# A linear-attention kernel and a maxout layer: two stages in turn, then one software pipeline

## The chip, the cores and the metric

The kernel runs on one core of one Trainium2 chip. The metric is the device time of one execution in microseconds (us), as the median of several executions. Profiles are single executions of the same kernel; their span is a few us shorter than the measured time. An execution counts as slow if it is over 1.5% above the fastest one of its kernel, and comparisons use fast runs alone.

Engines in the profile: PE is the TensorE (matmuls), PEld its weight loads, DVE the VectorE, ACT the ScalarE, POOL the GpSimd and SP the SyncE, which here only issues transfers. "Clock" is the share of its full speed that the record grants to the TensorE; the record is a list of entries, and the views count time without an entry as full (the kernel before has none until 215.3 us, and its attention reads 1.00).

## The reference

A gated linear attention over 4 batches, 8 heads, 768 positions and 48 elements a head, then a two-way maxout layer (384 to 1024 to 384) over the 3072 tokens.

```python
f = 1.0 / (1.0 + np.exp(-f_logit))
for t in range(S):                       # S = 768
    state = f[:, :, t, :, None] * state + einsum('bhd,bhe->bhde', k[:, :, t], v[:, :, t])
    y[:, :, t] = einsum('bhd,bhde->bhe', q[:, :, t], state)
x = y.transpose(0, 2, 1, 3).reshape(B * S, H * D)          # 3072 x 384
out = np.maximum(x @ w1, x @ w2) @ w_out                   # w1, w2: 384 x 1024
```

Both kernels cut the time axis into 6 chunks of 128 positions; a tile is one chunk of one batch with all heads, so there are 24 tiles. In a chunk the decays become cumulative sums (`cum`), q and k are scaled with their exponentials, and y is a masked product inside the chunk (`at`) plus q times the carried state; `sadd` updates the state.

## The kernel before

It has two stages. The first goes through the tiles (cut to the lines that the argument touches):

```python
for c in range(nch):
    for b in range(B):
        ...                                        # loads: q, k, f by SP, v by POOL (with a cast)
        nc.scalar.activation(tmp, ft2, AF.Exp, bias=0.0, scale=-1.0)
        nc.scalar.activation(ell_c, tmp, AF.Ln, bias=1.0, scale=1.0)
        nc.tensor.matmul(out=cumL, lhsT=ut, rhs=ell_c, start=True, stop=True)
        ...                                        # F_dec, F_inv: Exp of cumL; qp = q*F_dec, kp = k*F_inv on POOL
        for p in range(npiece):                    # 8 transposes
            nc.tensor.transpose(out=trq[:, p * C:(p + 1) * C], in_=qp[:, p * C:(p + 1) * C], identity=ident)
            ...
        nc.vector.tensor_copy(trSe, trq[0:D, :])       # even heads
        nc.vector.tensor_copy(trSo, trq[64:64 + D, :]) # odd heads, moved to partitions 0 to 47
        for j in range(H):
            nc.tensor.matmul(out=at_all[:, j, :], lhsT=kpT(j), rhs=qpT(j), start=True, stop=True)
        nc.vector.tensor_mul(at_m, at_all, ut_big)
        for j in range(H):
            nc.tensor.matmul(out=yps[:, ds], lhsT=at_m[:, j, :], rhs=v_c[:, ds], start=True, stop=False)
            nc.tensor.matmul(out=yps[:, ds], lhsT=qpT(j), rhs=state[:, j, :], start=False, stop=True)
        ...                                        # sadd, new state
        nc.scalar.copy(x_sbuf[:, ti, :], yps)
```

The second loads and casts the weights, transposes x in 72 pieces, and then:

```python
for ffb in range(FGRP):                            # 8
    for ts in range(ntsub):                        # 6 groups of 512 tokens
        ...                                        # h1 += w1.T x, h2 += w2.T x: 3 matmuls each, one PSUM buffer each
        nc.scalar.copy(gslc, h1)
        nc.vector.tensor_max(gslc, gslc, h2)
for i in range(n_tok_tiles):
    ...                                            # ops: 8 matmuls over gT and wo, copy, store
```

## Time and profile before

| | before |
|---|---|
| time, median of 3 (range) | 327.97 us (327.60 to 328.39) |
| span of the profiled run | 324.3 us |
| attention, weights and transposes, layer | 190.5, 21.5, 112.3 us |

The prediction below quotes the page's busy line, slices, stages and costliest groups. One view that it did not read closely is the list of groups on PE. Columns: line, engine and operation, output<-inputs, shapes, count; then busy us and mean ns of one; then the idle time before and its releaser.

```profile
L196 PE MATMUL h<-xT,w 128*128 128x512 bf16 x144 | 39.8, 387 | 0.3 <-DVE xT L183 0.3
...
L209 PE MATMUL ops<-wo,gT 128*128 128x384 bf16 x192 | 33.2, 326 | 0.0
L121 PE MATMUL trq<-ident,kp 128*128 128x128 bf16 x96 | 25.0, 313 | 3.2 <-POOL kp L106 3.2
...
L136 PE MATMUL at_all<-trSe 48*128 48x128 bf16 x96 | 22.7, 303 | 0.0
...
L94 PE MATMUL cumL<-ell_c,ut 128*128 128x384 bf16 x24 | 11.7, 487 | 30.1 <-ACT ell_c L91 25.5 <-ACT F_inv L99 4.5
```

A matmul's duration is longer than its share of the engine, since neighbours overlap (at_all lasts 0.31 us where starts lie 0.11 apart), but like can be compared with like. L94 and L209 are alike: both stream 384 columns in 128*128. One averages 487 ns in attention, the other 326 ns in the layer. The spacings that the prediction reads say the same: 0.107 us for 128 columns in attention, 0.216 for 512 in the layer, which is 0.84 ns a column against 0.42. So the array does not run alike in the two. This difference decides the case, and it stood in the profile beforehand.

### The profile page before, as it was taken

The numbers are of one execution on the slowest core, as the hardware profiler recorded it, in microseconds if no ns is written. First come the engines' busy times: TensorE is split into PE (matmuls) and PEld (weight loads), VectorE is DVE, ScalarE is ACT, GpSimd is POOL, SyncE is SP. The second block draws the span as 40 slices with busy tenths as digits, with TensorE's granted clock in tenths as the row PEclk, the third lists the DMA queues.
The fourth block names the chain that finished last, engine by engine and source line by source line (L and its number), as shares of the span: only waits on it lengthen the run. The fifth ranks groups of instructions, "written<-read, shape, count | busy, mean of one in ns | idle before, by whom it ended". The sixth has DMA issues, their size and how long they took to land.

```text
span 324.3 us, 4531 instructions
## 1 busy us (share of the span) xinstructions
PE 253.9 (78%) x1728; PEld 150.3 (46%) x1728; DVE 155.3 (48%) x267; ACT 148.7 (46%) x241; POOL 75.2 (23%) x93
## 2 busy tenths in 40 slices
PE   0258857967867697789879787688999998999995
PEld 0136635644555365456546554333333333345663
DVE  0145443645545365564546638934444444444442
ACT  3973668467927965784687010023333333330000
POOL 6353235432433351364434200000000000000000
PEclk9999999999999999999999999999999999999999
DMA  9947465856665687667674209500000000012443
GB/s 147 120 80 114 51 87 78 142 63 85 98 99 73 79 117 111 85 89 114 90 99 25 14 8 379 196 2 0 0 0 2 0 0 0 2 50 97 161 157 121
DMA packets 105156, 26.23 MB, mean 81 GB/s; under 512 B 100272, under 2 KB 104368, under 8 KB 105136
## 3 DMA queue, kind: packets, MB, share of 16 engines
q1 hardware_dynamic: 80176, 23.60, 31.8%
q0 software_dynamic: 24960, 2.36, 13.9%
q8 instruction: 13, 0.21, 0.3%
q14 instruction: 7, 0.06, 0.1%
HBM read 23.59 MB, written 4.72 MB: 87 GB/s over the span
## 4 chain that ended last, share of the span: by engine, by line
issue 37%; PE 30%; POOL 17%; DVE 12%; ACT 2%; DMA 1%; DVEq 0%; POOLq 0%; ACTq 0%
PE h L199 12%; PE ops L209 10%; DVE gT L203 8%; POOL kp L106 7%; POOL vt L81 6%; POOL qp L103 3%; PE h L196 3%; PE tps L182 2%; DVE xT L183 2%; PE yps L143 1%; PE yps L144 1%; DMA vt<-in_v_dram 1%; ACT L91 1%; POOL ut_big L51 1%; DVE wo L173 1%
## 5 line engine op out<-in xcount | busy, mean ns | idle before, releaser
L202 ACT CAST gT<-h 128x512 bf16<-128x512 f32 x48 | 28.1, 585 | 71.1 <-PE h L196 71.1
L203 DVE TENSOR_TENSOR gT<-gT,h 128x512 bf16<-128x512 bf16 x48 | 33.0, 687 | 48.0 <-PE h L199 48.0
L138 DVE TENSOR_TENSOR at_m<-at_all,ut_big 128x1024 bf16<-128x1024 f32 x24 | 29.4, 1224 | 43.7 <-PE at_all L136 43.7
L199 PE MATMUL h<-xT,w 128*128 128x512 bf16 x144 | 39.5, 382 | 7.4 <-DVE gT L203 7.4
L143 PE MATMUL yps<-vt,at_m 128*128 128x48 bf16 x192 | 42.8, 223 | 1.3 <-DVE at_m L138 1.3
L103 POOL TENSOR_TENSOR qp<-qt,F_dec 128x384 bf16<-128x384 f32 x24 | 23.7, 988 | 72.6 <-ACT F_dec L98 69.9
L196 PE MATMUL h<-xT,w 128*128 128x512 bf16 x144 | 39.8, 387 | 0.3 <-DVE xT L183 0.3
L94 PE MATMUL cumL<-ell_c,ut 128*128 128x384 bf16 x24 | 11.7, 487 | 30.1 <-ACT ell_c L91 25.5
L158 ACT CAST x_sbuf<-yps 128x384 bf16<-128x384 f32 x24 | 11.5, 477 | 50.0 <-PE yps L144 49.6
L209 PE MATMUL ops<-wo,gT 128*128 128x384 bf16 x192 | 33.2, 326 | 0.0
L91 ACT ACT_TABLE_LOAD x24 | 30.8, 1283 | 0.4
L81 POOL DMA_DIRECT2D vt<-in_v_dram x24 | 22.6, 941 | 34.5 <-PE yps L144 31.1
L149 PEld LDWEIGHTS <-kp 128*48 128x48 bf16 x192 | 9.7, 128 | 44.0 <-DMA vt<-in_v_dram 35.4
L124 DVE COPY trSe<-trq 48x1024 bf16<-48x1024 bf16 x24 | 16.4, 681 | 25.9 <-PE trq L121 25.9
L199 PEld LDWEIGHTS <-w 128*128 128x128 bf16 x144 | 14.1, 98 | 29.9 <-issue 18.4
L121 PE MATMUL trq<-ident,kp 128*128 128x128 bf16 x96 | 25.0, 313 | 3.2 <-POOL kp L106 3.2
L149 PE MATMUL sadd<-vt,kp 128*48 128x48 bf16 x192 | 12.7, 217 | 18.7 <-DMA vt<-in_v_dram 18.0
L143 PEld LDWEIGHTS <-at_m 128*128 128x128 bf16 x192 | 20.1, 105 | 12.0 <-DVE at_m L138 1.6
L106 POOL TENSOR_TENSOR kp<-kt,F_inv 128x384 bf16<-128x384 f32 x24 | 25.4, 1056 | 0.1
L152 DVE TENSOR_TENSOR tmpS<-state,sadd 48x384 f32<-48x384 bf16 x24 | 13.1, 546 | 25.1 <-PE sadd L149 24.9
L209 PEld LDWEIGHTS <-gT 128*128 128x128 bf16 x192 | 18.8, 98 | 13.7
L120 PE MATMUL trq<-ident,qp 128*128 128x128 bf16 x96 | 24.1, 303 | 0.0
(42 smaller groups left out, 370.6 us busy)
## 6 DMA issues: line engine op xcount, KB each, us to landing
qt<-in_q_dram SPq DMA_DIRECT2D x24, 192.0 KB, 2.7
kt<-in_k_dram SPq DMA_DIRECT2D x24, 192.0 KB, 3.2
ft<-in_f_logit_dram SPq DMA_DIRECT2D x24, 192.0 KB, 3.7
out_dram<-obuf SPq DMA_DIRECT2D x24, 192.0 KB, 1.9
w_f<-in_moe_w_dram SPq DMA_DIRECT2D x2, 1536.0 KB, 8.4
vt<-in_v_dram POOLq DMA_DIRECT2D x24, 96.0 KB, 3.7
wo_f<-in_moe_w_out_dram SPq DMA_DIRECT2D x1, 1536.0 KB, 14.1
```

The lines of the kernel that those rows point to most:

```text
L81: nc.gpsimd.dma_start(out=vt, in_=v[b, :, sl, :].rearrange("h p d -> p h d"))
L91: nc.scalar.activation(ell_c, tmp, AF.Ln, bias=1.0, scale=1.0)
L103: nc.gpsimd.tensor_mul(qp.rearrange("p (h e) -> p h e", h=H)[:, :, :D], q_c.rearrange("p (h d) -> p h d", h=H), F_dec.rearrange("p (h d) - ...
L106: nc.gpsimd.tensor_mul(kp.rearrange("p (h e) -> p h e", h=H)[:, :, :D], k_c.rearrange("p (h d) -> p h d", h=H), F_inv.rearrange("p (h d) - ...
L121: nc.tensor.transpose(out=trq[:, HDP + p * C:HDP + (p + 1) * C], in_=kp[:, p * C:(p + 1) * C], identity=ident)
L138: nc.vector.tensor_mul(at_m, at_all, ut_big)
L143: nc.tensor.matmul(out=yps[:, ds], lhsT=at_m[:, j, :], rhs=v_c[:, ds], start=True, stop=False)
L196: nc.tensor.matmul(out=h1, lhsT=w1[:, j, ffb * C:(ffb + 1) * C], rhs=xT[:, j, tslice], start=(j == 0), stop=(j == DGRP - 1))
L199: nc.tensor.matmul(out=h2, lhsT=w2[:, j, ffb * C:(ffb + 1) * C], rhs=xT[:, j, tslice], start=(j == 0), stop=(j == DGRP - 1))
L202: nc.scalar.copy(gslc, h1)
L203: nc.vector.tensor_max(gslc, gslc, h2)
L209: nc.tensor.matmul(out=ops, lhsT=gT[:, ffb, i * C:(i + 1) * C], rhs=wo[:, ffb, :], start=(ffb == 0), stop=(ffb == FGRP - 1))
```

## The change

The intent is one pipeline instead of two stages. A slot is one tile; in it PE makes `at` of tile n, y and the state of tile n-1, `cum` of tile n+2 and the transposes of tile n+1, and between them up to two pieces `d` of the layer (h for 128 of the 1024 columns and 512 tokens) and one piece `o` (the output of 128 tokens). The order on each engine is fixed by the program. With it come:

- maxout as `relu(x(w1-w2)) @ wo + x (w2 wo)`, which halves the h matmuls and drops the maximum; `w2 wo` (m2) is computed once, on PE;
- x made transposed by y's matmuls; heads 6 and 7 then lie in the wrong block, so w1 and w2 are loaded in a changed row order and six small copies per group of four tiles move the rows of x;
- heads in pairs on partitions 0 to 63 and 64 to 127 (zero-padded), and one preloaded activation table.

```diff
-        # attention stage, then weights and x's transposes, then the layer
+    nc.scalar.preload_act_table_set("natural_log_exp_and_others")
+    def load_rows(dst, w):                       # w1, w2 in the row order of x
+        hd = w.rearrange("(h d) f -> d h f", d=D)
+        nc.sync.dma_start(out=dst[0:D, :, :], in_=hd[:, 0:6:2, :])
+        nc.sync.dma_start(out=dst[DP:DP + D, :, :], in_=hd[:, 1:6:2, :])
+        for r in range(2):
+            ...                                  # 16 partitions each
+    def stage_A_pe(n):
+        for j in range(NP):
+            for r in range(2):
+                rows = slice(r * DP, r * DP + D)
+                nc.tensor.matmul(out=ps[r][:, j, :], lhsT=t[rows, 0, j, :], rhs=t[rows, 1, j, :],
+                                 start=True, stop=True)
+    def stage_Y_act(n):
+        nc.scalar.copy(xT[c][:, :, b * C:(b + 1) * C], ys.pop(n))
+        if b == B - 1:
+            for r in range(2):
+                for i in range(KT):              # six copies of 16 partitions
+                    nc.sync.dma_start(out=x[r * DP + D:(r + 1) * DP, i, :],
+                                      in_=x[r * DP + 16 * i:r * DP + 16 * (i + 1), KT, :])
+    def piece_d(g, ff):
+        ...                                      # 3 matmuls into h
+        nc.scalar.activation(gT[g][:, ff, :], ps, AF.Relu)
+    def piece_o(g, b):
+        ...                                      # 3 matmuls with m2, then 8 with wo
+    slot = -3
+    while slot < n_tiles + 2 or queue:
+        n = slot
+        if n % B == 1 and 4 < n <= n_tiles + 1:  # layer pieces of a finished group
+            g = (n - 5) // B
+            queue += [("d", g, ff) for ff in range(FG)] + [("o", g, b) for b in range(B)]
+        ...                                      # load(n+5), E(n+3), A(n), Y(n-1), D(n-1), C(n+2),
+        ...                                      # one d, T(n+1), one d, one o
```

In the prediction "mode" means the rows by columns of the array that a matmul uses, as the timeline prints them (48*128, 128*128, ...); each change of it is put at the 0.13 us more that the prediction reads between at_all and trq.

> **What bounds the kernel now.** I read first the busy time of each engine and the slices on the page, then the table by stage, then the groups, and last the timeline for the spacing of matmuls. From the page, busy time and the slices (tenths busy, each 8.1 us):
>
> ```profile
> PE 253.9 (78%) x1728; PEld 150.3 (46%) x1728; DVE 155.3 (48%) x267; ACT 148.7 (46%) x241; POOL 75.2 (23%) x93
> ...
> PE   0258857967867697789879787688999998999995
> ...
> ACT  3973668467927965784687010023333333330000
> POOL 6353235432433351364434200000000000000000
> ...
> DMA  9947465856665687667674209500000000012443
> GB/s 147 120 80 114 51 87 78 142 63 85 98 99 73 79 117 111 85 89 114 90 99 25 14 8 379 196 2 0 0 0 2 0 0 0 2 50 97 161 157 121
> ```
>
> PE is the busiest, yet not filled, and three regimes follow one another: attention (to slice 23), where ACT, POOL and DMA work; weights and transposes of x (24 to 26); the layer, where DMA is idle. The stage table (stretch, its length, busy us of each engine, clock, DMA share, GB/s) says how long each is:
>
> ```profile
> 21.80:190.50 168.70, 132.18 (x1115) 90.60 (x1115) 89.73 (x117) 105.03 (x171) 63.73 (x65) 1.00 0.63 85
> 190.50:212.00 21.50, 15.40 (x88) 9.26 (x89) 16.63 (x75) 0.48 (x1) 0.00 (x0) 1.00 0.60 220
> 212.00:290.00 78.00, 70.54 (x297) 29.14 (x298) 31.92 (x49) 26.92 (x46) 0.00 (x0) 1.00 0.02 6
> 290.00:324.30 34.30, 30.65 (x185) 17.79 (x183) 14.21 (x25) 1.17 (x2) 0.00 (x0) 1.00 0.35 127
> ```
>
> Attention takes 168.7 us for 23 tiles, 7.3 each, and no engine is full in it: ACT 62%, PE 78% by spans that overlap. It is bound by waits around short buffers (the largest by pairs of engine: POOL's qp for F_dec on ACT 69.9 us, ACT's x_sbuf for yps 49.6, DVE's at_m for at_all 43.7, POOL's issue of v for yps 31.1). The groups show what fills ACT, and the two evacuations of the layer:
>
> ```profile
> L203 DVE TENSOR_TENSOR gT<-gT,h 128x512 bf16<-128x512 bf16 x48 | 33.0, 687 | 48.0 <-PE h L199 48.0
> L143 PE MATMUL yps<-vt,at_m 128*128 128x48 bf16 x192 | 42.8, 223 | 1.3 <-DVE at_m L138 1.3
> L91 ACT ACT_TABLE_LOAD x24 | 30.8, 1283 | 0.4
> ```
>
> With the smaller groups (16, 6 and 3) there are 49 table loads, 62.9 us, 42% of ACT's busy time. In the timeline (start, duration) starts tell what a matmul really takes, since durations overlap:
>
> ```profile
> 179.57 0.22 PE L144 MATMUL yps<-state,trSo 48*128 48x48 bf16 x1
> 179.72 0.22 PE L143 MATMUL yps<-vt,at_m 128*128 128x48 bf16 x1
> 179.88 0.22 PE L144 MATMUL yps<-state,trSe 48*128 48x48 bf16 x1
> ...
> 182.06 0.31 PE L136 MATMUL at_all<-trSe 48*128 48x128 bf16 x1
> 182.17 0.31 PE L136 MATMUL at_all<-trSo 48*128 48x128 bf16 x1
> 182.41 0.29 PE L120 MATMUL trq<-ident,qp 128*128 128x128 bf16 x1
> ```
>
> So yps costs 0.153 us a matmul where weights of 128 and of 48 rows alternate, although it streams 48 columns; at_all, all of one kind, costs 0.107 with 128 columns; a change of kind (at_all to trq) costs 0.24, some 0.13 more. By the same reading sadd takes 0.056 each (8 in 0.45), h 0.216 (3 in 0.65) and ops 0.1625 (8 per 1.30 us). In the layer one round of h1 and h2 takes 1.655 us for 1.29 of matmuls: each PSUM buffer of h is single and PE waits for its evacuation.
>
> [...]exp and ln are both in natural_log_exp_and_others, so one load serves both;[...] the input streams at 147 GB/s with DMA full (slice 0), the weights at 379. The change leaves that.
>
> **The change, part by part.** *Removed:* 48 of 49 table loads, about 61.6 us of ACT; 144 matmuls of h (144 x 0.216 = 31 us of PE); 48 maxima (33 us of DVE); 72 transposes and copies of x (7.7 us of PE at 0.107); the serial stage of 21.5 us; the alternation in y; v's issue on POOL. *Added:* x times m2 inside o, 72 x 0.1625 = 11.7 us of PE; preparation of w2T and m2, 24 x 0.107 + 24 x 0.1625 = 6.5 us; wd on POOL: kp takes 1.0 us for 384 elements, so 3072 take about 8 us, once. *Moved:* both regimes are interleaved in one order per slot (a slot is one tile). The listing of the changed order gives, for a full slot on PE:
> - transposes 8 x 0.107 = 0.86; at 8 x 0.107 = 0.86;
> - y 16 x 0.08 = 1.28 (estimate between sadd's 0.056 and at's 0.107, for 64 weight columns and 128 streamed); sadd 8 x 0.06 = 0.5;
> - cum 0.16 plus four sums of about 0.1 = 0.56;
> - d 6 x 0.216 = 1.30; o 11 x 0.1625 = 1.79;
> - four changes of mode, 4 x 0.13 = 0.5.
>
> Sum 7.65. The even and odd heads now sit on different rows of the array and may overlap, worth up to 0.6 in at and y; I choose **7.4 us**. Beside it ACT needs 2 x 0.52 + 0.59 + 2 x 0.485 + 0.17 + 2 x 0.585 = 3.9, DVE two at_m halves of 0.69, trs 0.69, tmp_s 0.4, vb 0.3, ob 0.56 = 3.3, POOL 2.05 + 0.7 = 2.8, DMA 786 KB at 150 GB/s = 5.2 plus the output's 0.5. So PE sets the steady slot, and results are used a slot later than made[...]; I expect few waits there.
>
> The start is set by DMA. Four tiles lie ahead of the weights: 4 x 5.2 + 2 = 23 us. The weights, 4.7 MB, take 13 us at the 379 GB/s of before; in the new row order pieces of 48 and 16 partitions may be slower, I take 17. So f of tile 4 lands at about 41; slot 1 hangs there, because ACT runs the slot's Exp before the copies behind it. From there a tile lands each 5.2 us: slot 5 starts at about 58, loses about 4 to m2 (3.9) and to wd on POOL, ahead of kp of tile 6; slots 5 to 7 have no o and take 10, 6, 6. Slot 8 starts at about **86**. Slots 8 to 24: 17 x 7.4 = 126, less 6 since the last four lack sadd, and then cum, transposes, at: **120**. The tail, layer only: four slots of two d and one o (3.1) and three of one o (1.8) = **18**. After the last matmul, 3.7 as now (320.6 to 324.3). Sum 228; the measured time lies 3.7 above the span (327.97 against 324.3): 231.5. I add 2.5 for waits not seen: **234 us**.
>
> **The rivals.** *DMA is the bound throughout:* 24 x 5.2 + 17 + 4.7 MB of output at about 350 GB/s (13) = 155 us plus the tail; under PE's sum, but if small packets go slower in company (85 GB/s at share 0.63 is 135 at full, so 5.8 a tile) the start slips by some 6 us: about 240. *A fixed order turns into waits* (PE blocked on a bank that ACT frees late, ACT blocked behind an Exp that waits for f): nothing is that close in the sums, ACT being half filled; one wait of 0.5 us per slot would give 245, one of 1 us 255. *Modes cost more than I take:* if y and at in 64-row and 64-column tiles run at 0.15 as yps did, a slot gains 1.5 us: 258. *Heads overlap fully* (0.055 each for at and y): slot 6.7, time 222. *The start hides better*, weights at full rate: 229.
>
> **Range and chances.** Slot 7.4 with 0.6 either way is 10 us, the start 7, and waits only add: 218 to 256. Even the worst rival lies 20% under 328, so faster by over 2% is 0.98.
>
> **What would show it.** ACT has one table load; busy ACT about 95 us. PE slices are low up to about 40 us with DMA near full, then 9s from about 85 us to the tail. Starts of the first at_e of successive slots lie 7.0 to 7.8 apart in the middle; at_e to at_o spacing tells about overlap (0.107 or 0.055), the step from Y to sadd and cum about modes. wd on POOL shows 7 to 8 us. The chain that ended last should be PE from o, d and y, with DMA at its beginning. The prediction is wrong if the slots in the middle are paced by something other than PE, if the weights take over 25 us, or if matmuls in small tiles space wider than 0.11.

## The result, and the profile after

| | before | after |
|---|---|---|
| time, median of 4 (range) | 327.79 us (327.54 to 328.39) | 206.52 us (206.28 to 206.89) |
| ratio of fast runs | | 0.6302 (95%: 0.6279 to 0.6325) |
| span of the profiled run | 324.3 us | 204.9 us |
| PE busy | 253.9 us | 141.6 us |

A ratio is the mean time of one kernel's fast runs over the mean of the other's fast runs of the same rounds, so it is not quite the ratio of the medians. The changed kernel is 37% faster, and at 206.5 us it lies below the predicted range of 218 to 256. A later repeat of the unaltered file, beside a later batch of runs, gave 206.81 us (206.14 to 209.44), ratio 0.631.

The page of the changed kernel, busy time and slices (tenths; each slice 5.1 us):

```profile
PE 141.6 (69%) x1452; PEld 85.7 (42%) x1472; DVE 81.6 (40%) x145; ACT 87.6 (43%) x196; POOL 72.3 (35%) x90
...
PE   0257300004464999929999699995999999959993
...
PEclk9999999999999799975999979997999999979999
DMA  6999999999999499958699589795891111111122
GB/s 126 189 186 191 162 163 168 228 242 198 186 187 187 72 187 185 171 97 172 141 176 217 116 167 179 150 224 107 168 196 45 58 42 40 45 55 38 55 95 80
```

There are two regimes: to slice 12 the DMA is full and PE mostly waits; afterwards PE is full apart from four dips. Each dip has a fall of the granted clock beside or after it. Stages of the changed kernel (stretch, length, busy of PE, PEld, DVE, ACT, POOL, clock, DMA share, GB/s; the last two rows are one steady slot and one of the long ones):

```profile
13.19:81.58 68.39, 31.50 (x368) 21.15 (x372) 29.10 (x44) 23.99 (x60) 25.91 (x21) 0.98 1.14 181
...
122.19:127.23 5.04, 4.99 (x63) 3.13 (x64) 3.04 (x6) 3.49 (x8) 2.57 (x3) 1.00 0.87 174
86.62:98.10 11.48, 7.35 (x63) 3.94 (x64) 3.04 (x6) 3.60 (x8) 2.56 (x3) 0.70 0.71 137
```

**The steady slot takes 5.04 us, not 7.4.** Its timeline on PE (start, duration, operation; from the second half of `at`):

```profile
122.31 0.22 PE L178 MATMUL at_e<-trs 48*128 48x128 bf16 x1
122.32 0.22 PE L178 MATMUL at_o<-trs 48*128 48x128 bf16 x1
122.37 0.22 PE L178 MATMUL at_e<-trs 48*128 48x128 bf16 x1
122.37 0.22 PE L178 MATMUL at_o<-trs 48*128 48x128 bf16 x1
122.52 0.41 PE L200 MATMUL y<-trs,state 48*64 48x128 bf16 x8
122.86 0.41 PE L205 MATMUL y<-at_m,vb 128*64 128x128 bf16 x8
123.11 0.29 PE L218 MATMUL sadd<-vb,kp 128*64 128x64 bf16 x8
123.33 0.34 PE L127 MATMUL cum<-ell,ut 128*128 128x384 bf16 x1
...
124.25 0.39 PE L160 MATMUL trp<-ident,kp 128*128 128x128 bf16 x4
124.47 0.39 PE L160 MATMUL trp<-ident,qp 128*128 128x128 bf16 x4
```

Read the starts. Four transposes of 128 columns take 124.47 - 124.25 = 0.22 us, 0.056 each, where the kernel before took 0.107. The starts of successive at_e are also 0.055 apart, each with an at_o beside it. Early in the same run, before the layer joins in, both were slow:

```profile
66.05 0.31 PE L178 MATMUL at_e<-trs 48*128 48x128 bf16 x1
66.06 0.31 PE L178 MATMUL at_o<-trs 48*128 48x128 bf16 x1
66.16 0.31 PE L178 MATMUL at_e<-trs 48*128 48x128 bf16 x1
66.16 0.31 PE L178 MATMUL at_o<-trs 48*128 48x128 bf16 x1
```

Here at_e starts are 0.11 apart and a matmul lasts 0.31 us instead of 0.22: the durations of the kernel before. The mean clock does not show this: it is 0.98 over this first stage and 1.00 over all attention of the kernel before. Most of that time has no entry in the record and is counted as full. In the packed traces the entries begin at 62.5 us here, and in the kernel before only at 215.3 us, 3.2 us after the first h. Where there is an entry, the spacing fits it: 66.05 lies in one of half rate (65.9 to 69.3), and in this run all 111 gaps between transposes under full entries are 55 or 56 ns, all 21 under half entries 106 or 107.

In this run the entries and the spacings agree, then: 106 to 107 ns for 128 columns at half rate, 55 to 56 at full. What misleads is the mean.

**Three slots of the steady part are long**, 11.5, 9.0 and 9.1 us (9.4, 9.0 and 8.8 in the later repeat). The first of them on PE:

```profile
87.93 0.24 PE L130 MATMUL cum<-ones_col,ell 128*128 128x1 bf16 x4
92.04 1.87 PE L258 MATMUL h<-xT,wd 128*128 128x512 bf16 x3 [3.87 <-DMA xT<-xT]
93.70 0.63 PE L160 MATMUL trp<-ident,kp 128*128 128x128 bf16 x4
94.13 0.63 PE L160 MATMUL trp<-ident,qp 128*128 128x128 bf16 x4
```

and what SP, which issues the transfers, did at that time:

```profile
85.93 0.99 SPq L71 DMA_DIRECT2D vt<-in_v_dram  x1
87.02 4.98 SPq L249 DMA_DIRECT2D xT<-xT  x6
```

PE stops 3.87 us for the six copies of xT that the piece `d` needs, and the matmuls after it run at half rate again (four transposes in 0.43 us). SP reaches the copies only after the loads of tile 13, and issuing the six takes it 4.98 us, against a median of 1.9 us from the issue of a copy to its landing.

**The start.** On ACT, the wait for the first input behind the weights ends at 45.36:

```profile
45.36 0.52 ACT L120 ACTIVATE tmp_e<-ft 128x384 f32<-128x384 f32 x1 [26.91 <-DMA ft<-in_f_logit_dram]
```

Slots 1 and 2 begin at 17.38 and 21.48, so a tile lands each 4.1 us, at the page's 186 to 191 GB/s. The weights, which the slices show at 160 to 170 and at last 240 GB/s, hold the queue from about 21 to 44 us: 23 us.

### The profile page after: what moved, and what is told of

The parts are those of the page before. It is cut to its first block, busy times and chain, and to the rows that moved or that the text cites. A ratio compares the mean times of both kernels' runs of the same rounds, so it can differ in the third digit from the quotient of the medians.

```text
span 204.9 us, 3795 instructions
## 1 busy us (share of the span) xinstructions
PE 141.6 (69%) x1452; PEld 85.7 (42%) x1472; DVE 81.6 (40%) x145; ACT 87.6 (43%) x196; POOL 72.3 (35%) x90
## 4 chain that ended last, share of the span: by engine, by line
PE 52%; issue 19%; SPq 9%; DMA 8%; DVE 5%; ACT 3%; POOL 2%; DVEq 0%; POOLq 0%
PE h L258 15%; PE o L268 13%; PE o L265 5%; SPq L249 5%; PE trp L160 4%; SPq L71 4%; DMA xT<-xT 4%; PE at_e L178 3%; PE y L205 3%; PE y L200 3%; PE m2p L295 2%; DMA ft<-in_f_logit_dram 2%; DMA qt<-in_q_dram 2%; PE cum L127 2%; DVE vb L153 1%
## 5 line engine op out<-in xcount | busy, mean ns | idle before, releaser
L258 PE MATMUL h<-xT,wd 128*128 128x512 bf16 x124 | 41.7, 413 | 12.2 <-DMA xT<-xT 10.3
L260 ACT ACTIVATE gT<-h 128x512 bf16<-128x512 f32 x48 | 28.9, 603 | 31.2 <-PE h L258 30.7
L147 POOL TENSOR_TENSOR kp<-kt,f_inv 128x384 bf16<-128x384 f32 x24 | 24.9, 1037 | 39.6 <-ACT f_inv L140 36.0
L168 DVE COPY trs<-trp 128x1024 bf16<-128x1024 bf16 x24 | 16.6, 691 | 54.3 <-PE trp L160 54.3
L268 PE MATMUL o<-wo,gT 128*128 128x384 bf16 x192 | 35.1, 326 | 0.0
L244 ACT CAST xT<-y 128x512 bf16<-128x512 f32 x24 | 14.0, 582 | 29.4 <-PE y L205 29.4
L149 POOL TENSOR_TENSOR qp<-qt,f_dec 128x384 bf16<-128x384 f32 x24 | 24.0, 1000 | 0.0
L186 DVE TENSOR_TENSOR at_m<-at_e,ut 128x512 bf16<-128x512 f32 x24 | 16.4, 685 | 5.7 <-PE at_o L178 5.7
L265 PE MATMUL o<-m,xT 128*128 128x384 bf16 x72 | 16.7, 344 | 0.0
L186 DVE TENSOR_TENSOR at_m<-at_o,ut 128x512 bf16<-128x512 f32 x24 | 16.3, 681 | 0.0
## 6 DMA issues: line engine op xcount, KB each, us to landing
w_f<-in_moe_w_dram SPq DMA_DIRECT2D x4, 576.0 KB, 13.2
```

The lines of the kernel that those rows point to most:

```text
L147: nc.gpsimd.tensor_mul(padded["kp"][n % NB][:, :, 0:D], loaded[n]["k"], f_inv.rearrange("p (h d) -> p h d", h=H))
L149: nc.gpsimd.tensor_mul(padded["qp"][n % NB][:, :, 0:D], loaded[n]["q"], f_dec.rearrange("p (h d) -> p h d", h=H))
L168: nc.vector.tensor_copy(t, ps)
L186: nc.vector.tensor_mul(m[:, r], ps[r], ut4)
L244: nc.scalar.copy(xT[c][:, :, b * C:(b + 1) * C], ys.pop(n))
L258: nc.tensor.matmul(out=ps, lhsT=wd[:, kt, ff * C:(ff + 1) * C], rhs=xT[g][:, kt, :], start=(kt == 0), stop=(kt == KT - 1))
```

## The experiments

The experiments ran in four batches, in which the kernel before took 326.6 to 327.87 us (medians), so each is given with its ratio to the kernel before in the same rounds; for the changed kernel that is 0.6302 and 0.631. "Slot lengths" are differences between the starts of the first at_e of successive tiles in the timeline. The theory after the result was: the spacings that the prediction took from attention were half-rate spacings, and the dense order of the changed kernel runs at full rate. The rival: the new operations (padded pairs, other tiles, another order) are cheaper in themselves.

### All layer pieces after attention (e1)

```diff
-        p = next_piece(n, "d")
+        p = next_piece(n, "d") if n > n_tiles else None     # likewise for "o"; six xT buffers
```

> The changed kernel with all layer pieces moved behind the attention (same instructions, not interleaved; xT gets six buffers). Theory 'clock': [...]it stays at half rate as in the kernel before and in the first 66 us of the changed kernel: transposes 0.106 us apart, a pair of even and odd heads of at 0.105, a 384-column matmul shown as about 0.48. Rival 'shape of the tiles': the fast spacing comes from the new tiles, so transposes stay at 0.056 and pairs of at at 0.055 in attention too. In both, attention is paced by the input at about 4.1 us a tile, ends near 135 us, and the layer adds 48 x 0.65 + 24 x 1.79 = 74 us: about 216 us in all, 4% slower than the changed kernel.

Measured: 235.1 us (231.95 to 236.67), ratio 0.7148. The attention operations are the very ones of the changed kernel, now without the layer between them. Clock in slices and a timeline of PE in attention:

```profile
PEclk9999999999988755555555555559999999999999
```

```profile
102.35 0.59 PE L160 MATMUL trp<-ident,kp 128*128 128x128 bf16 x4
102.72 0.64 PE L160 MATMUL trp<-ident,qp 128*128 128x128 bf16 x4
104.15 0.28 PE L178 MATMUL at_e<-trs 48*128 48x128 bf16 x1 [0.79 <-DVE trs L168]
```

The spacing is back at 0.105 for 128 columns, the record itself grants half, and slots take 4.13 us, the pace at which inputs land. So the operations are not cheaper in themselves; they are cheaper in dense company: PE is busy for 16.08 of 20 us here (80 to 100 us), against 4.99 of 5.04 in the steady slot. The expected total was missed, because attention ended only at 154 us: slot 8 began at 83.5, and sixteen slots of 4.13 us or more follow. Interleaving, by overlap and density together, is worth 29 us here.

### The kernel before with useless matmuls (e7)

```diff
                 yps = ps_y.tile([C, HD], F32, name="yps")
+                for _ in range(12):                          # 384 columns each, overwritten afterwards
+                    nc.tensor.matmul(out=yps, lhsT=ut, rhs=ut_big[:, 0:3, :]..., start=True, stop=True)
```

> The kernel before with twelve extra matmuls of 384 columns a tile into the bank of yps, which the first real matmul overwrites; the result stays right. Theory 'clock': PE is then busy enough for the full rate, transposes and at go from 0.107 to 0.056 apart, the extra matmuls take 0.1625 each, and the time stays near 327 (315 to 335) despite 288 more matmuls. Rival 'shape': the spacing stays 0.107, the extra ones take 0.32 each, and 24 x 3.8 us come on top: 400 or more.

Measured: 323.45 us (319.9 to 328.41), ratio 0.9869 (0.9808 to 0.9931). The groups on PE, the fillers first:

```profile
L142 PE MATMUL yps<-ut_big,ut 128*128 128x384 bf16 x288 | 72.1, 385 | 0.4 <-ACT F_last L115 0.3
...
L136 PE MATMUL at_all<-trSe 48*128 48x128 bf16 x96 | 17.4, 234 | 0.0
L121 PE MATMUL trq<-ident,kp 128*128 128x128 bf16 x96 | 16.9, 233 | 1.9 <-POOL kp L106 1.7
```

288 more matmuls, and the kernel is not slower: PE is 90% busy instead of 78%, a transpose of k takes 233 ns instead of 313, at_all 234 instead of 303, and in the timeline both are spaced 0.056 us wherever the record's entry is full, about 0.107 where it is half. The tiles, pools and shapes of the kernel before are untouched, so this refutes the rival and shows the clock's part. Two limits of it: the alternating yps matmuls went only from 0.153 to 0.127 us, so most of that cost is not the clock, and that it is the change of tile shape, which the prediction named, is the author's reading, which no run separates (in the changed kernel y no longer alternates, and its 16 take 0.59 us); and the time gained by the clock went into the fillers, so e7 is a proof and no remedy.

### Odd heads on the rows of even ones (e10), and even heads first (e2)

These ask what the two row halves are worth. e10 gives wrong results on purpose.

```diff
-                rows = slice(r * DP, r * DP + D)
+                rows = slice(0, D)                           # e10: both heads read rows 0 to 47
```
```diff
-        for j in range(NP):
-            for r in range(2):
+        for r in range(2):                                   # e2: also in y and sadd
+            for j in range(NP):
```

> Wrong result on purpose: the odd heads of at and of the state part of y read the rows of the even heads, so that all eight matmuls of a group stand on the same rows of the array[...]; e2 failed to show this, since the two row groups ran side by side whatever their order. Theory 'clock': at comes at 0.056 a matmul instead of 0.055 a pair, which adds 0.2 us a slot, y's state part 0.1: slots of 5.3, time up by 4 to 6 us. Rival 'overlap was the larger miss': slots over 6 us, time over 225.

> The changed kernel with all four even heads first and then the four odd ones in at, y and sadd, so that neighbouring matmuls lie on the same rows or columns of the array[...]. Theory 'clock': with the clock up the matmuls of at come at 0.056 each instead of 0.055 a pair, which adds 0.2 us a slot for at and 0.1 to 0.2 each for both parts of y and for sadd: a slot goes from 5.04 to about 5.6, the time to about 215. Rival 'overlap is what I mis-sized': slots go to 7 us, the time to about 240. If the time does not move, overlap is worth nothing.

e10: 206.91 us, ratio 0.6306 (0.6271 to 0.6341). With common rows the eight are 0.056 apart instead of in pairs (timeline of PE in e10):

```profile
122.17 0.23 PE L178 MATMUL at_e<-trs 48*128 48x128 bf16 x1
122.24 0.22 PE L178 MATMUL at_o<-trs 48*128 48x128 bf16 x1
122.29 0.22 PE L178 MATMUL at_e<-trs 48*128 48x128 bf16 x1
```

The slot takes 5.26 us, 0.22 more. The time stays the same all the same, since the long slots shrank (9.1, 7.5 and 8.5 us, against 9.4, 9.0 and 8.8 in the repeat of the same batch); that longer slots leave the copies more time is likely but not shown. So running side by side on different rows is worth 0.22 us a slot, all of it in `at`, and explains little. e10 leaves the column halves of y and sadd as they are, so what those are worth was not tested.

e2: 208.26 us, ratio 0.6352 (0.6311 to 0.6393), slot 5.08. It failed as an experiment: in program order all four at_e now come before the at_o, but PE still ran them in pairs (timeline of PE in e2):

```profile
110.18 0.23 PE L178 MATMUL at_e<-trs 48*128 48x128 bf16 x1
110.20 0.23 PE L178 MATMUL at_o<-trs 48*128 48x128 bf16 x1
110.25 0.22 PE L178 MATMUL at_e<-trs 48*128 48x128 bf16 x1
110.26 0.22 PE L178 MATMUL at_o<-trs 48*128 48x128 bf16 x1
```

### The other parts of the change: tables (e3, e5) and maxout (e4)

```diff
-    nc.scalar.preload_act_table_set("natural_log_exp_and_others")      # e3: after without it; e5: before with it
```
```diff
-        nc.scalar.activation(gT[g][:, ff, :], ps, AF.Relu)             # e4
+        ...                                                            # a second group ps2 with w2; no m2, wd = w1
+        nc.scalar.copy(gT[g][:, ff, :], ps)
+        nc.vector.tensor_max(gT[g][:, ff, :], gT[g][:, ff, :], ps2)
```

> The changed kernel without its preload of the common table: 49 table loads as before, two a tile. Theory: in a slot of 5.04 us ACT is busy 3.9 us, with two loads of 1.28 it needs 6.5, becomes the bound, and slots go to 6.5 to 7: about 232 us. Rival: the loads fall into ACT's idle time and the pipeline hides them: under 211.

> The kernel before with the common table preloaded, so 1 load instead of 49. Theory: two loads, 2.6 us, lie in the chain of each tile of 7.3 us; attention falls towards what PE needs at its slow spacing (about 5.7 us a tile): 285 to 300 us. Rival: the loads are hidden behind other waits: over 320.

> The changed kernel with the maximum taken as before: h1 and h2 both multiplied, copied by ACT and compared by DVE, no m2. Theory: PE in a slot gains 6 x 0.215 and loses 3 x 0.1625, so 5.04 goes to 5.84, and the preparation of m2 (some 6 us) goes: about 214 to 218. Rival: slots have that much slack while the input sets the pace, 205 to 210. Second rival: DVE, now with 4.7 us a slot, and ten banks a slot bring waits: over 225.

e3: 216.77 us, ratio 0.6568. The 49 loads come back and ACT's busy time goes from 87.6 to 147.2 us, yet only 10 us are lost, fewer than expected: where PE has layer work, slots go in pairs of 5.04 and of about 7 us, and ACT is 19.6 to 19.8 us busy in stretches of 20, so ACT nearly sets the pace. e5: 310.34 us, ratio 0.948, so one table alone takes 17 us off the kernel before, also fewer than expected; attention ends at 178.1 instead of 190.5 us in its trace, though 61 us of ACT are gone. In both, most of the loads lay beside other waits. e4: 217.31 us, ratio 0.6634, slot 5.84: six more matmuls of h less three of m2 are 6 x 0.216 - 3 x 0.1625 = 0.81 us, as reckoned, a hit. The relu form is worth 0.8 us a slot and 11 us in all.

### The copies of xT: another queue (e6), later layer pieces (e9, e13), none at all (e16)

```diff
-                    nc.sync.dma_start(out=x[r * DP + D...                # e6
+                    nc.scalar.dma_start(out=x[r * DP + D...
```
```diff
-        if n % B == 1 and 4 < n <= n_tiles + 1:                          # e9: pieces one slot later
-            g = (n - 5) // B
+        if n % B == 2 and 5 < n <= n_tiles + 2:
+            g = (n - 6) // B
+        # e13: two slots later (n % B == 3, n - 7), and four xT buffers
```
```diff
-        if b == B - 1:                                                   # e16: no copies
+        if False:
```

> The changed kernel with the six small copies that spread xT issued by ACT instead of SP. Theory: they wait behind two tiles of input on the one queue, so on another queue they land within about 3 us; slots 10, 14 and 18 (11.5, 9.0 and 9.1 us) come down to 5 to 6, the end gains some 3 us, and the time falls by 12 to 16 us to about 192. Rival: the 16 DMA engines are full whichever queue is used, and the copies land as late as now: 204 to 208.

> The changed kernel with each group's layer pieces begun one slot later. Theory: in three of the slots PE waits for the six copies that spread xT (11.5, 9.0 and 9.1 us in place of 5.04: 14.5 us in all, part of it the wait and part slow matmuls after it) and once more at the end; with 5 us more of slack these waits and the slow stretches behind them vanish, the tail gains one slot of 3.1 us: 190 to 196 us. Rival: the slots are paced by the input (4.1 us of DMA a tile and the output), so what is saved there is waited for elsewhere: 203 to 208.

> The layer pieces of a group start two slots later than in the changed kernel (one more than in e9), with four xT buffers instead of three. Theory (the long slots are PE waiting for the six xT copies, each followed by a stretch at a slow clock): no wait of PE on xT of over 0.3 us before the tail is left, the three long slots of e9 (6.0, 9.3, 6.4 us) go to 5.0 to 5.5, worth 6 us, and the tail grows by one slot without attention (about 2 us): 191 to 196 us, ratio near 0.59. Rival (what is left of the long slots in e9 comes from the clock or from late inputs and not from the copies): no change against e9, 196 to 198 us.

> Wrong result on purpose: the six copies that bring the last 16 rows of each head pair to the other blocks of xT are left out (the rows hold zeros). It prices what the copies cost as they stand. Theory: the three slots of 11.5, 9.0 and 9.1 us go to 5.0 to 5.3, worth 14 us, and the tail from 25 to about 20 us: 187 to 191 us. Rival (the copies only uncover another wait, such as f landing late, since inputs then are wanted faster): only half of it, 196 to 200 us, with ACT waiting longer for ft in the slots that were long.

e6 was a miss: 213.41 us, ratio 0.6534. Six issues cost ACT 3.73 us (SP 4.98), and ACT is needed (timeline of ACT in e6):

```profile
84.05 0.57 ACT L244 CAST xT<-y 128x512 bf16<-128x512 f32 x1
84.65 3.73 ACTq L249 DMA_DIRECT2D xT<-xT  x6
88.48 0.49 ACT L140 ACTIVATE f_inv<-cum 128x384 f32<-128x384 f32 x1 [3.86 <-DMA xT<-xT]
```

The copies go out sooner, but the relus come late and PE's `o` waits for gT instead (9.9 us between 81 and 170).

e16, wrong on purpose, prices the copies: 189.83 us (189.45 to 190.54), ratio 0.5789, with slots 8 to 22 all at 4.6 to 5.04 us. Against the changed kernel that is 16.7 us, the whole of the long slots and of the stall in the tail. The rival, that another wait would appear in their place, is refuted.

e9 keeps the result right: 197.18 us (195.23 to 198.24), ratio 0.6003 (0.5964 to 0.6041), faster than both kernels and 1 us above the expected range, since the waits shrank but did not vanish. PE's waits in the steady part (81 to 170 us), after, then e9:

```profile
PE h L258 <- DMA xT<-xT: 7.9, 4, 3.9
```

```profile
PE h L258 <- DMA xT<-xT: 3.2, 6, 1.7
```

(us in total, times, longest.) e13, two slots later: 195.69 us (194.43 to 196.72), ratio 0.5975 (0.5951 to 0.5999), within the interval of e9, so the two are not told apart. PE has no wait for xT left between 88 and 170 us, as the theory said; but in the same view of ACT the inputs took its place:

```profile
ACT tmp_e L120 <- DMA ft<-in_f_logit_dram: 21.7, 10, 4.5
```

In the changed kernel ACT has no such wait in that stretch. The early slots of e13 have no layer work and take 3.5 to 3.8 us, so they use up the loads that lay ahead, and then slots wait for inputs. e9 and e13 are the best versions with a right result; the remaining 6 to 7 us to e16 were not won.

### Loads four tiles ahead instead of five (e12)

```diff
-    AHEAD = 5
+    AHEAD = 4
```

> The changed kernel with loads issued four tiles ahead instead of five. Theory: the xT copies start late because SP first has to issue the loads of the tile five ahead[...]; with four ahead SP reaches the copies about 4 us earlier, the three long slots shrink to about 6, and the time falls by 8 to 14 us. Rival: the copies' own issue (0.6 us each) and landing are the wait, and the time stays within 3 us.

209.93 us (207.09 to 210.5), ratio 0.6361 (0.6313 to 0.6409): the theory missed and the rival came true, since the interval overlaps that of the unaltered repeat (0.6283 to 0.6337) and the two are not told apart. The profiled run was a slow one, so only with care: its first long slot was shorter (6.3 us), the later ones longer (11.8 and 12.0).

### The weights: two queues (e8), and all 128 partitions (e15)

```diff
-            nc.sync.dma_start(out=dst[r * DP + D:(r + 1) * DP, :, :], in_=rows)      # e8: odd rows by ACT
+            (nc.sync, nc.scalar)[r].dma_start(out=dst[r * DP + D:(r + 1) * DP, :, :], in_=rows)
```
```diff
+        nc.sync.dma_start(out=dst, in_=w.rearrange("(j p) f -> p j f", p=C))         # e15: plain row order
+        return
```

> The changed kernel with the odd heads' rows of w1 and w2 loaded through ACT's queue beside the even ones on SP's. Theory: the weights took 23 us (21 to 44) because pieces of 48 and 16 partitions went one after another[...]; side by side they need some 15, tile 4 lands 6 to 8 us earlier, and the time is about 199. Rival: the DMA engines are the bound and only the order of landing changes: 205 to 209.

> Wrong result on purpose: w1 and w2 are loaded in one transfer each over 128 partitions in the plain row order of the kernel before, instead of four transfers over 48 and 16 partitions. Theory (the weights took 23 us and not the 17 predicted because transfers over few partitions are slow): the weights take 13 to 14 us, f of tile 4 lands about 9 us earlier, slot 8 starts at 71 to 74 instead of 81.6, and the time is 196 to 199 us. Rival (the start is bound by the inputs of tiles 4 to 8 and by PE's work and not by the weights' transfers): time 204 us or more.

e8 tested nothing: 211.89 us, ratio 0.6466. ACT issued its half at the very start, ahead of the first tiles, so slot 0 began at 28.6 instead of 13.2 us and the halves never ran together.

e15, wrong on purpose: 197.58 us (195.99 to 198.33), ratio 0.6017 (0.5988 to 0.6046), inside the expected 196 to 199. Its GB/s slices and the same wait on ACT:

```profile
GB/s 124 189 186 208 408 385 240 195 187 186 187 121 137 194 169 175 104 151 198 177 199 96 173 199 178 196 66 151 154 94 51 56 41 42 56 49 41 81 81 81
```

```profile
33.48 0.52 ACT L122 ACTIVATE tmp_e<-ft 128x384 f32<-128x384 f32 x1 [15.11 <-DMA ft<-in_f_logit_dram]
```

The same bytes run at 385 to 408 GB/s instead of 160 to 170, f of tile 4 comes 11.9 us earlier, and slot 8 begins at 70.0 instead of 81.6. e15 changes partitions, size and number of transfers together (128 partitions and 1536 KB each, against 48 and 16 partitions and 576 and 192 KB) and does not separate them. So the new row order of the weights costs 9 us. A load that has both the order and the speed was not tried.

### The changed kernel again

> The changed kernel unaltered, beside the next three on their chip, as their yardstick: 205 to 209 us, steady slots of 5.04 us.

206.81 us (206.14 to 209.44): the yardstick of its batch, quoted above.

## Why the prediction was wrong

The direction was right and the size was not. This is its sum against the profile, in us:

| term | predicted | measured | difference |
|---|---|---|---|
| slot 8 begins | 86 | 81.6 | -4.4 |
| slots 8 to 24 | 120 | 97.6 (81.6 to 179.2) | -22.4 |
| tail to the last matmul | 18 | 22.2 (to 201.4) | +4.2 |
| to the end of the span | 3.7 | 3.5 | -0.2 |
| span to time | 3.7 | 1.6 | -2.1 |
| unseen waits | 2.5 | 0 | -2.5 |
| sum | 233.9 | 206.5 | -27.4 |

**The step that failed** is the slot's list: "transposes 8 x 0.107 = 0.86; at 8 x 0.107 = 0.86; y 16 x 0.08 = 1.28 (...); sadd 8 x 0.06 = 0.5; cum 0.16 plus four sums of about 0.1 = 0.56". Apart from cum's 0.16, a full-rate figure that held (0.17), these rest on attention of the kernel before, which ran at half rate (0.107 us for 128 columns, the spacing under half entries). The five terms took 0.45, 0.33, 0.59, 0.22 and 0.28: 1.87 us in place of 4.06, with "four changes of mode, 4 x 0.13 = 0.5" already inside them, which makes 4.56 against 1.87. Of this difference some 0.5 is matmuls side by side, of which the prediction allowed 0.25: 0.22 in `at` by e10, and an estimated 0.3 in y, whose 16 would take 16 x 0.056 = 0.90 one by one. The rest is mostly the rate. The two terms read from the layer, where the record's entry is full from 215.3 us on, held: d 1.29 for 1.30, o 1.88 for 1.79. e1 and e7 show that density is what moves the spacing. The text had the contradiction in hand: it had read 0.216 us for 512 columns and 0.1625 for 384 in the layer, 0.42 ns a column, which would give some 54 ns for 128 (an estimate), and took 107 from attention as what a matmul "really takes", beside a clock of 1.00 that stood for no entry. It then multiplied a spacing from a sparse stage into a dense one.

**The second step that failed** goes the other way and hid part of the first. Of the "fixed order turns into waits" rival it said "nothing is that close in the sums". The change's list of additions had no term at all for the six copies of xT, neither SP's time to issue them nor a transfer that PE must wait for one slot later. The slot alone would have put slots 8 to 24 at 17 x 5.04 = 85.7; the three long slots add 14.5, and the last slots, with less work, give back 2.6: 97.6. In the tail the same wait costs 2.2 us, and with the slow clock after it (half rate in the record from 182.0 to 185.4 us) most of the 4.2; the tail's own units, 3.1 and 1.8, held. e16 prices all of it at 16.7 us. So this rival was true, though it was outweighed.

**The start** came out close by two errors. "4 x 5.2 + 2" supposed 150 GB/s for inputs; they run at 186 to 191, 4.1 us a tile. "I take 17" for the weights was a guess in the right direction: 23. f of tile 4 landed at about 45, not 41. Slots 3 to 5 then took 7.4, 7.7 and 8.8 us, held by the casts and copies of the weights on DVE, by wd and by m2, and slots 6 and 7 only 3.5 each.

**The other rivals.** "DMA is the bound throughout" holds up to about 50 us (slot 3) and not beyond: from there inputs land each 4.2 us, while slots 3 to 5 take 7.4 to 8.8. (Its 350 GB/s for the output was the author's estimate, and no run shows it.) "Modes cost more" is refuted: at and y space narrower than even the low estimate. "Heads overlap fully" is true of `at` in the trace, but worth some 0.5 us a slot with y (0.22 measured, the rest estimated above) rather than 0.7, on costs that had halved already. Of the signs named, one table load (1283 ns) and PE full from about 85 us, but for the long slots, came true, and ACT near 95 (87.6) and wd at 7 to 8 us (6.7) nearly; "7.0 to 7.8" between slots did not. None of the three conditions under which the text called itself wrong was met in the steady slots (PE sets their pace, the weights took 23 us, at and y space below 0.11), so they could not have caught the error.

## What to carry to other kernels

A matmul's spacing belonged to the density of its stage here (PE busy 80% at half rate in e1, 99% at full rate in the steady slot): compare the time per column in a sparse and in a dense stretch (0.84 and 0.42 ns here) before multiplying it into a new schedule, and do not take a mean clock of 1.00 as proof where the record has no entries. A stall of PE cost more than its length here, since the matmuls after it ran slowly (3.9 us of waiting made a slot 6.4 us longer, with four transposes in 0.43 us instead of 0.22). List every transfer between two stages, however small, with its issue time and its place in the issuing queue, and give its consumer one more slot of slack; here that gave 9 us.
